# Attention inside a fused block: value products in five visits per group, six banks for the scores, and one bank with fixed places for the rest

## The chip, the cores and the metric

The kernel runs on one core of a Trainium2 chip. The metric is the device time of one execution in microseconds (us). Engines are named as the profile names them: PE is TensorE's matmuls, PEld its weight loads, DVE is VectorE, ACT is ScalarE, POOL is GpSimd and SP is SyncE, which here issues nearly all DMA transfers.

## The reference

One layer over x of shape (1, 2048, 448) computes two branches and mixes them by a gate, all in float32.

```
x = A_x
g = sigmoid((x * gate_w).sum(-1))
a = attention(x): q = x @ wq (16 heads of 28), k = x @ wk, v = x @ wv (one head, shared by all)
    p = softmax(q k^T * 28**-0.5);  o = p v;  a = o @ wo
b = mixer(x): x1 = x + shift(gelu(layernorm(x) @ w1)) @ w2
    b = x1 + gelu(layernorm(x1) @ w3) @ w4
out = g * a + (1 - g) * b
```

## The kernel before

The kernel has three stages. The first projects k and v, computes q for the first two groups, and makes the first half of the mixer. The second is the rest of the mixer, with 56 hidden tiles. Both end some 420 us into the execution and aren't touched by the change. The third is attention, and the change lies there.

**Groups.** The 2048 queries fall into NB = 4 blocks of 512, and the 16 heads into NG = 4 sets of four. A pair of block and set is a group, u = 0 to 15. A group walks NT = 16 key tiles of 128 keys. For each key tile and each of its four heads, one matmul makes scores, keys by queries, 128 x 512, in a PSUM bank (L662), and ScalarE takes the exponential into an SBUF tile p (L664). There are 64 such steps in a group, and this text calls them slots 0 to 63: slot 4 kt + j is head j of key tile kt.

**Value products.** `pv_group(k)` (L617) multiplies the four p tiles of one key tile with the values. Four matmuls, each with 32 output rows, stand side by side in TensorE's array, one per head, and accumulate in one PSUM bank, mx, over the whole group. The weights have a column of ones, so that one output row per head is the softmax's sum. The score loop goes on for two key tiles (LAG = 2) before it does the products of two earlier key tiles in a row (PVB = 2). Such a stretch of value products is called a visit. There are eight visits in a group.

**Other TensorE work of a group**, all between the scores:

- q projection: `q_job(u + 2)` (L492), eleven matmuls of 128 x 512, started in group u at key tile 2. `q_evac` (L144) rounds the result into qh (on ScalarE) and takes the rest ql (on VectorE), and three DMA transfers of 256 KB write qh, ql and qh again into rows 0 to 95 of the tile qs, from which both scores and maxima are made.
- row maxima of a sample of the scores, for group u + 1: `max_part` (L161) four times, each with four matmuls of 128 columns and one reduce on VectorE; they read rows 0 to 95 of qs. `max_end` (L182) and `max_rows` (L190) turn the result, with one matmul and a copy on ScalarE, and two transfers write it into rows 96 and 97 of qs.
- normalisation of the group before: `recip_begin` (L522) copies o out of PSUM on ScalarE, sends the sums through a DMA to a tile rt, checks and inverts them on VectorE, and sends the result back through two DMA transfers (rb). `norm_job` (L540) spreads rb by one matmul, rbc, and multiplies; POOL splits the product into onh and onl.
- the output projection wo: after the fourth group of a block, `wo_job` (L566) runs once for each of its four tiles of 128 queries, with twelve matmuls into one bank, and `gate_out` (L561) applies the gate and stores the tile. For the last block, `wo_last_job` (L638) keeps four banks open in the last group.

These jobs are generators. `pump()` (L600) runs them one matmul at a time after every second score, in the order of the list `jobs`, so where each matmul lands depends on what lies ahead of it in the list. The maxima have fixed places, behind key tiles 6 to 9 and 11.

**Banks.** PSUM has eight banks. Scores rotate over five (mm 2, misc 1, s 2), the value products have one (mx), and the other work has two (m). In the last group the scores use three, because the four open output banks take the rest.

**What sets the order.** PE's order is that of the code: the kernel declares it hand-written (L59). The order on the other engines and of the DMA issues is the compiler's: it takes what it expects to be ready, in the order of the code where several are. Semaphores and the buffers (`bufs`) then decide when something runs. All DMA transfers named here are issued by SyncE on one queue.

```
            if k >= LAG and k % PVB == PVB - 1:
                for kk in range(k - LAG - PVB + 1, k - LAG + 1):
                    if kk >= 0:
                        pv_group(kk)
```

Of the kernel before, what the change touches and what calls it, by code (L numbers as in the profile page):

```python
# [29 lines left out]
LAG = 2  # L30
PVB = 2
# [9 lines left out]
def gated_mix_kernel(  # L41
# [102 lines left out]
    def q_evac(pool, u, ps, qs):  # L144
        qh = pool.tile([P, 512], F32R, tag="qh", bufs=2 if pool.name == "s1" else 1, name=f"qh_{u}")
        ql = pool.tile([P, 512], F32R, tag="ql", bufs=2 if pool.name == "s1" else 1, name=f"ql_{u}")
        nc.scalar.copy(qh, ps)
# [42 lines left out]
    def max_rows(u, tile_of):  # L190
# [4 lines left out]
        nc.scalar.copy(mrow, ps[0:32, :])  # L195
# [196 lines left out]
    with tc.tile_pool(name="s2", bufs=1, reuse_waits="tile") as s2, \  # L392
            tc.tile_pool(name="ps2", bufs=1, space=PSUM, reuse_waits="tile") as ps2:
        fills = [lambda t=t: max_part(0, t, max_tile) for t in range(4)]
        fills += [lambda: max_end(0), lambda: None, lambda: None, lambda: max_rows(0, max_tile)]
# [57 lines left out]
    with tc.tile_pool(name="s3", bufs=1, reuse_waits="tile") as s3, \  # L453
# [23 lines left out]
        def s_tile(n, last=False):  # L477
            return (mm_tile, mm_tile, s_spare, s_more, s_more)[n % (3 if last else 5)](f"s_{n}")
# [13 lines left out]
        def q_job(u):  # L492
# [15 lines left out]
            yield  # L508
# [31 lines left out]
        def norm_job(u, o, rb):  # L540
            ps = (mm_tile if u == NU - 2 else misc_tile)(f"rbc_{u}")
# [3 lines left out]
            onh = s3.tile([P, 512], F32R, tag="onh", bufs=5, name=f"onh_{u}")  # L545
            onl = s3.tile([P, 512], F32R, tag="onl", bufs=5, name=f"onl_{u}")
# [3 lines left out]
            yield  # L550

        def wo_group(ps, b, t, g, first, last):
            tok = slice(t * P, (t + 1) * P)
            onh, onl = on_of[b * NG + g]
            nc.tensor.matmul(ps, onh[:, tok], woh[:, g, :], start=first, stop=False)  # L555
# [3 lines left out]
            nc.tensor.matmul(ps, onl[:, tok], woh[:, g, :], start=False, stop=last)  # L559

        def gate_out(n, ps):  # L561
            ot = s3.tile([P, D], F32, tag="ot", bufs=3, name=f"ot_{n}")
            nc.vector.scalar_tensor_tensor(ot, ps, gg[:, n:n + 1], x1[:, n, :], op0=ALU.mult, op1=ALU.add)  # L563
            nc.sync.dma_start(out[0, n * P:(n + 1) * P, :], ot)

        def wo_job(b, t):  # L566
            ps = misc_tile(f"wo_{b}_{t}")[:, 0:D]
            for g in range(NG):
                yield from wo_group(ps, b, t, g, g == 0, g == NG - 1)
                if g < NG - 1:  # L570
                    yield
            gate_out(4 * b + t, ps)
            yield
# [26 lines left out]
        def pump():  # L600
            if current[0] is None:
                if jobs:
                    current[0] = jobs.pop(0)()
                    next(current[0])
            else:
                try:
                    next(current[0])
                except StopIteration:
                    current[0] = None

        def drain():
            while current[0] is not None or jobs:
                pump()

        p_of, pv_of = {}, {}

        def pv_group(k):  # L617
# [8 lines left out]
            if kt == NT - 1 and u < NU - 1:  # L626
                o, rb = recip_begin(u, pv_of.pop(u))
                delayed.append((k + 6, lambda: norm_job(u, o, rb)))
                if u == NU - 2:
                    for t in range(4):  # L630
                        delayed.append((k + 10, lambda t=t: wo_last_job(t, NG - 2)))
                elif u % NG == NG - 1:
                    for t in range(4):
                        delayed.append((k + 8, lambda t=t: wo_job(u // NG, t)))

        wo_last = []

        def wo_last_job(t, g):  # L638
            if g == 0:
                wo_last.append((m_tile if t < 2 else s_more)(f"wo_{NB - 1}_{t}")[:, 0:D])  # L640
            yield from wo_group(wo_last[t], NB - 1, t, g, g == 0, False)
            yield

        delayed = []
        for k in range(NU * NT + LAG):
            u, kt = divmod(k, NT)
            while delayed and delayed[0][0] <= k:
                jobs.append(delayed.pop(0)[1])
            if k == (NU - 1) * NT:
                for g in range(NG - 2):  # L650
                    for t in range(4):
                        jobs.append(lambda t=t, g=g: wo_last_job(t, g))
            if k < NU * NT:
                if kt == (7 if u == 0 else 2) and u + 2 < NU:
                    jobs.insert(0, lambda u=u: q_job(u + 2))
                if kt == 8 and (u + 3) % NG == 0 and u + 3 < NU:
                    load_x((u + 3) // NG)
                p_of[k] = []
                for j in range(4):
                    n = 4 * k + j  # L660
                    ps = s_tile(n, u == NU - 1)
                    nc.tensor.matmul(ps, kS[0:98, kt * P:(kt + 1) * P], q_of[u][0:98, j, :], start=True, stop=True)  # L662
                    p = s3.tile([P, 512], F32, tag="p", bufs=4 * (LAG + PVB) + 2, name=f"p_{n}")
                    nc.scalar.activation(p, ps, AF.Exp, scale=SCALE)  # L664
                    p_of[k].append(p)
                    if j % 2 == 1 or u == NU - 1:
                        pump()
                if u + 1 < NU:
                    if 6 <= kt < 10:
                        max_part(u + 1, kt - 6, m_tile)  # L670
# [138 lines left out]
```

## Time and profile before

| | |
|---|---|
| median of the runs shown | 1069.96 us (3 runs, 1068.99 to 1070.19) |
| the profiled execution | 1067.96 us, span 1066.2 us |
| first score of the attention stage | 420.57 us into the span |
| first and last copy of o (groups 0 and 14) | 466.4 and 1011.3 us |
| mean granted TensorE clock | 0.987 |
| busy: PE, ACT, DVE, POOL | 98%, 63%, 24%, 14% of the span |

The profile gives one line per group of instructions or, in the timeline, per run of equal instructions: start, duration, engine, line of the code, operation, the tile written and the tiles read, and the count. In brackets stand the idle time of the engine before it and what ended that. Matmuls overlap, so a matmul's duration (0.40 us for 128 x 512) is longer than the distance to the next one. A busy PE is therefore no proof that nothing waits; the distances between starts are. A weight load (PEld) that waits shows a wait of TensorE. In tables of stages the columns are the stretch, its length, the busy time of PE, PEld, DVE, ACT and POOL with their counts, the granted clock, the busy share of the DMA engines and GB/s.

### The profile page before, as it was taken

The numbers are of one execution on the slowest core, as the hardware profiler recorded it, in microseconds if no ns is written. First come the engines' busy times: TensorE is split into PE (matmuls) and PEld (weight loads), VectorE is DVE, ScalarE is ACT, GpSimd is POOL, SyncE is SP. The second block draws the span as 40 slices with busy tenths as digits, with TensorE's granted clock in tenths as the row PEclk, the third lists the DMA queues.
The fourth block names the chain that finished last, engine by engine and source line by source line (L and its number), as shares of the span: only waits on it lengthen the run. The fifth ranks groups of instructions, "written<-read, shape, count | busy, mean of one in ns | idle before, by whom it ended". The sixth has DMA issues, their size and how long they took to land.

```text
span 1066.2 us, 13945 instructions
## 1 busy us (share of the span) xinstructions
PE 1040.3 (98%) x5610; PEld 679.5 (64%) x5610; DVE 258.6 (24%) x528; ACT 673.5 (63%) x1318; POOL 146.1 (14%) x175
## 2 busy tenths in 40 slices
PE   7999989999999999999999999999999999999996
PEld 4787878888888887454554555554655555555442
DVE  6734862411412212301110110120110210111102
ACT  5444462222222223798888888889888888888873
POOL 5622200200200202602000002020002010000100
PEclk8899999999999999999999999999999999999998
DMA  9501330000000001323211202220202220202001
GB/s 312 133 1 37 112 111 1 1 1 1 1 1 1 1 1 61 132 32 70 32 18 15 31 19 41 39 31 3 39 10 41 39 31 2 40 21 30 10 2 38
DMA packets 30541, 41.15 MB, mean 39 GB/s; under 512 B 8004, under 2 KB 20100, under 8 KB 30340
## 3 DMA queue, kind: packets, MB, share of 16 engines
q1 hardware_dynamic: 30324, 40.04, 16.2%
q8 instruction: 46, 0.75, 0.3%
q14 instruction: 27, 0.22, 0.1%
q10 hardware_dynamic: 144, 0.13, 0.0%
HBM read 23.28 MB, written 3.67 MB: 25 GB/s over the span
## 4 chain that ended last, share of the span: by engine, by line
PE 92%; DVE 2%; DMA 2%; ACT 1%; POOL 1%; issue 1%; SPq 0%; POOLq 0%; DVEq 0%; ACTq 0%
PE s L662 27%; PE pv L624 22%; PE acc L418 4%; PE acc L419 4%; PE acc L420 4%; PE g L115 4%; PE g L116 4%; PE g L117 4%; PE q L502 3%; PE m L166 2%; PE wo L559 1%; PE wo L557 1%; PE g L119 1%; PE wo L555 1%; PE g L118 1%; PE h L116 1%
## 5 line engine op out<-in xcount | busy, mean ns | idle before, releaser
L664 ACT ACTIVATE p<-s 128x512 f32<-128x512 f32 x1024 | 517.6, 630 | 99.7 <-PE s L662 99.4
L662 PE MATMUL s<-qs,kS 98*128 98x512 f32 x1024 | 343.5, 420 | 1.4 <-ACT p L664 0.7
L662 PEld LDWEIGHTS s<-qs,kS 98*128 98x128 f32 x1024 | 181.7, 189 | 168.3 <-ACT p L664 126.2
L624 PE MATMUL pv<-p,vext 128*32 128x512 f32 x2048 | 247.5, 601 | 0.0
L408 ACT ACTIVATE gh<-g 128x512 fp32r<-128x512 f32 x56 | 33.6, 599 | 175.0 <-PE g L119 174.9
L624 PEld LDWEIGHTS pv<-p,vext 128*32 128x32 f32 x2048 | 53.7, 109 | 107.5 <-issue 100.1
L410 DVE TENSOR_TENSOR gl<-gf,gh 128x512 fp32r<-128x512 f32 x56 | 38.7, 692 | 183.8 <-ACT gf L409 183.8
L418 PE MATMUL acc<-w4h,gh 128*128 128x448 f32 x224 | 82.8, 370 | 0.0
L419 PE MATMUL acc<-w4l,gh 128*128 128x448 f32 x224 | 82.0, 366 | 0.0
L420 PE MATMUL acc<-w4h,gl 128*128 128x448 f32 x224 | 81.7, 365 | 0.0
L167 DVE TENSOR_REDUCE mr<-m 128x4 f32<-128x512 f32 x64 | 44.2, 691 | 146.8 <-PE m L166 146.1
L115 PE MATMUL g<-ah,w3h 128*128 128x512 f32 x168 | 66.6, 396 | 3.7 <-ACT gf L409 3.7
L116 PE MATMUL g<-al,w3h 128*128 128x512 f32 x168 | 66.3, 395 | 0.0
L117 PE MATMUL g<-ah,w3l 128*128 128x512 f32 x168 | 66.3, 394 | 0.0
L547 POOL CAST onh<-on 128x512 fp32r<-128x512 f32 x15 | 9.2, 614 | 415.0 <-DVE on L544 228.9
L520 DVE SCALAR_TENSOR_TENSOR good<-rt,good 128x16 f32<-128x16 f32 x15 | 2.6, 175 | 190.9 <-DMA rt<-o 190.9
L418 PEld LDWEIGHTS acc<-w4h,gh 128*128 128x128 f32 x224 | 42.2, 188 | 4.9
L419 PEld LDWEIGHTS acc<-w4l,gh 128*128 128x128 f32 x224 | 42.2, 188 | 4.9
L420 PEld LDWEIGHTS acc<-w4h,gl 128*128 128x128 f32 x224 | 42.0, 188 | 3.6
L166 PEld LDWEIGHTS m<-kS,qs 96*128 96x128 f32 x256 | 38.4, 191 | 6.3 <-DVE mr L167 1.2
L115 PEld LDWEIGHTS g<-ah,w3h 128*128 128x128 f32 x168 | 31.7, 188 | 9.9 <-ACT gf L409 4.1
L563 DVE SCALAR_TENSOR_TENSOR ot<-wo,gg,x 128x448 f32<-128x448 f32 x16 | 10.9, 681 | 108.0 <-PE wo L559 107.9
(204 smaller groups left out, 1134.9 us busy)
## 6 DMA issues: line engine op xcount, KB each, us to landing
qs<-qh SPq DMA_DIRECT2D x32, 256.0 KB
qs<-ql SPq DMA_DIRECT2D x16, 256.0 KB
xq<-in_xT_dram SPq DMA_DIRECT2D x4, 1024.0 KB
x<-in_x_dram SPq DMA_DIRECT2D x4, 896.0 KB
w3raw<-in_w_dram SPq DMA_DIRECT2D x7, 512.0 KB
out_dram<-ot SPq DMA_DIRECT2D x16, 224.0 KB
w4raw<-in_w_dram SPq DMA_DIRECT2D x7, 448.0 KB
xkv<-in_xT_dram SPq DMA_DIRECT2D x3, 1024.0 KB
```

Source lines behind the costliest of these rows:

```text
L115: nc.tensor.matmul(ps, wh[:, c, :], ah[:, c, :], start=(c == 0), stop=False)
L116: nc.tensor.matmul(ps, wh[:, c, :], al[:, c, :], start=False, stop=False)
L117: nc.tensor.matmul(ps, wl[:, c, :], ah[:, c, :], start=False, stop=False)
L166: nc.tensor.matmul(ps[:, j, :], q_of[u][0:96, j, t * P:(t + 1) * P], kS[0:96, 0:MK], start=True, stop=True)
L167: nc.vector.reduce_max(mx_of[u][:, :, t], ps, axis=AX.X)
L410: nc.vector.tensor_sub(gl, gf, f32(gh))
L418: nc.tensor.matmul(ps, gh[:, tok], w4h[i][:, k, :], start=(f == 0), stop=False)
L419: nc.tensor.matmul(ps, gh[:, tok], w4l[i][:, k, :], start=False, stop=False)
L420: nc.tensor.matmul(ps, gl[:, tok], w4h[i][:, k, :], start=False, stop=(f == NF - 1))
L624: nc.tensor.matmul(pv[32 * j:32 * j + 32, :], vext[:, kt, :], ps[j], start=(kt == 0), stop=(kt == NT - 1), tile_position=(0, 32 * j))
L662: nc.tensor.matmul(ps, kS[0:98, kt * P:(kt + 1) * P], q_of[u][0:98, j, :], start=True, stop=True)
L664: nc.scalar.activation(p, ps, AF.Exp, scale=SCALE)
```

## The change

The attention stage gets a new order of TensorE's work, new owners for the PSUM banks, and a new place for the output projection.

- Visits: five in a group in place of eight. Behind key tile 0 the last four key tiles of the group before are multiplied, and behind key tiles 3, 6, 9 and 12 three each. In the last group two more visits of two tiles follow, behind key tile 14 and at the end. Twenty-two p tiles in place of eighteen.
- Banks: scores rotate over six banks in every group (mm 2, misc 1, s 3). All other work shares one bank, m.
- Fixed places, by slot: rbc at 16; maxima of the next group at 19, 23, 27 and 35, their rows at 45; the twelve wo matmuls of the group before at 29 to 31, 39 to 41, 47 to 49 and 52 to 54; the q projection of the group after the next at 58, 60, 62 and 63 and, in the next group, at 0 to 3, 5, 7 and 9. Group 0 has its own places.
- q projection: with that, the last q matmul for group u + 1 and its evacuation stand in group u, at slot 9, and the first maximum of group u + 1 at slot 19 of the same group. Before, q of group u + 1 was done in group u - 1.
- Output projection: `wo_job` now runs for every group, three matmuls per query tile, and VectorE adds the gated product to a tile ot that lives over the four groups of a block (five buffers). The store follows the fourth. The last block has no banks of its own any more; in the tail, the first two query tiles share the m bank.
- The copies of q to qh and of the maxima's rows to mrow move from ScalarE to VectorE. The load of the next block's x stands at key tile 3 of the group in which its first q projection starts.

```diff
-            if k >= LAG and k % PVB == PVB - 1:
-                for kk in range(k - LAG - PVB + 1, k - LAG + 1):
-                    if kk >= 0:
-                        pv_group(kk)
+        WO_AT = (29, 30, 31, 39, 40, 41, 47, 48, 49, 52, 53, 54)
+        Q_AT = (58, 60, 62, 63, 0, 1, 2, 3, 5, 7, 9)
+        FIRST_AT = tuple(range(36, 58, 2))
+        M_AT = (19, 23, 27, 35, 45)
+        FIRST_M = (3, 7, 11, 15, 23)
+
+        visits = {0: (-4, 0), 3: (0, 3), 6: (3, 6), 9: (6, 9), 12: (9, 12)}
+        for k in range(NU * NT + 1):
+            u, kt = divmod(k, NT)
+            if k < NU * NT:
+                if kt == (9 if u == 0 else 14) and u + 2 < NU:
+                    jobs.append(q_job(u + 2))
+                if kt == 7 and u > 0:
+                    for t in range(4):
+                        jobs.append(wo_job(u - 1, t))
+                if kt == 3 and (u + 2) % NG == 0 and u + 2 < NU:
+                    load_x((u + 2) // NG)
...
+                    at = 4 * kt + j
+                    if at in (WO_AT + Q_AT if u else FIRST_AT):
+                        pump()
+                    if at == 16 and norms:
+                        norm(*norms.pop())
+                    places = M_AT if u else FIRST_M
+                    if u + 1 < NU and at in places:
+                        t = places.index(at)
+                        if t < 4:
+                            max_part(u + 1, t, m_tile)
+                        else:
+                            max_rows(u + 1, m_tile, nc.vector.tensor_copy)
+                        if t == 3:
+                            max_end(u + 1)
+            lo, hi = visits.get(kt, (0, 0))
+            if u == NU - 1 and kt == 14:
+                lo, hi = 12, 14
+            if u == NU:
+                lo = -2
+            for kk in range(u * NT + lo, u * NT + hi):
+                if kk >= 0:
+                    pv_group(kk)
...
         def m_tile(name):
-            return ps3.tile([P, 512], F32, tag="m", bufs=2, name=name)
+            return ps3.tile([P, 512], F32, tag="m", bufs=1, name=name)
 
         def s_more(name):
-            return ps3.tile([P, 512], F32, tag="s", bufs=2, name=name)
+            return ps3.tile([P, 512], F32, tag="s", bufs=3, name=name)
...
-        def s_tile(n, last=False):
-            return (mm_tile, mm_tile, s_spare, s_more, s_more)[n % (3 if last else 5)](f"s_{n}")
+        def s_tile(n):
+            return (mm_tile, mm_tile, s_spare, s_more, s_more, s_more)[n % 6](f"s_{n}")
...
-        nc.scalar.copy(qh, ps)
+        (nc.scalar.copy if pool.name == "s1" else nc.vector.tensor_copy)(qh, ps)
...
+        def wo_job(u, t, tile_of=misc_tile):
+            b, g = divmod(u, NG)
+            n = 4 * b + t
             tok = slice(t * P, (t + 1) * P)
+            onh, onl = on_of[u]
+            ps = tile_of(f"wo_{u}_{t}")[:, 0:D]
+            nc.tensor.matmul(ps, onh[:, tok], woh[:, g, :], start=True, stop=False)
             yield
             nc.tensor.matmul(ps, onh[:, tok], wol[:, g, :], start=False, stop=False)
             yield
+            nc.tensor.matmul(ps, onl[:, tok], woh[:, g, :], start=False, stop=True)
+            before = x1[:, n, :] if g == 0 else ot_of[n]
+            if g == 0:
+                ot_of[n] = s3.tile([P, D], F32, tag="ot", bufs=5, name=f"ot_{n}")
+            nc.vector.scalar_tensor_tensor(ot_of[n], ps, gg[:, n:n + 1], before, op0=ALU.mult, op1=ALU.add)
+            if g == NG - 1:
+                nc.sync.dma_start(out[0, n * P:(n + 1) * P, :], ot_of[n])
```

More of the change, by code (lines that the diff above doesn't have):

```diff
@@ L29 @@
 SHIFTS = (-1, 1, -2, 2)
-LAG = 2
-PVB = 2
+PB = 22
 MK = 128
@@ L194, in max_rows @@
         mrow = keep.tile([32, P], F32R, tag="mrow", bufs=2, name=f"mrow_{u}")
-        nc.scalar.copy(mrow, ps[0:32, :])
+        copy(mrow, ps[0:32, :])
         for k in range(2):
@@ L544, in norm_job @@
             nc.vector.tensor_mul(on, o, ps)
[L545 to L546 removed]
+            onh = s3.tile([P, 512], F32R, tag="onh", bufs=2, name=f"onh_{u}")
+            onl = s3.tile([P, 512], F32R, tag="onl", bufs=2, name=f"onl_{u}")
             nc.gpsimd.tensor_copy(onh, on)
@@ L549, in norm_job @@
             on_of[u] = (onh, onl)
-            yield
-        def wo_group(ps, b, t, g, first, last):
+        ot_of = {}
+        def wo_job(u, t, tile_of=misc_tile):
+            b, g = divmod(u, NG)
+            n = 4 * b + t
             tok = slice(t * P, (t + 1) * P)
-            onh, onl = on_of[b * NG + g]
-            nc.tensor.matmul(ps, onh[:, tok], woh[:, g, :], start=first, stop=False)
+            onh, onl = on_of[u]
+            ps = tile_of(f"wo_{u}_{t}")[:, 0:D]
+            nc.tensor.matmul(ps, onh[:, tok], woh[:, g, :], start=True, stop=False)
             yield
@@ L600, in pump @@
         def pump():
[L601 to L608, printed above, removed]
+            if jobs or current[0]:
+                current[0] = current[0] or jobs.pop(0)
+                if next(current[0], "done") == "done":
                     current[0] = None
[L611 to L615, printed above, removed]
+        p_of, pv_of, norms = {}, {}, []
         def pv_group(k):
```

85 lines of the change are left out of this document (17 added, 68 removed).

## The prediction

> **What bounds the kernel now.** I read the page first: busy shares, then the chain that ended last.
>
> ```profile
> span 1066.2 us, 13945 instructions
> ...
> PE 1040.3 (98%) x5610; PEld 679.5 (64%) x5610; DVE 258.6 (24%) x528; ACT 673.5 (63%) x1318; POOL 146.1 (14%) x175
> ...
> PE 92%; DVE 2%; DMA 2%; ACT 1%; POOL 1%; issue 1%; SPq 0%; POOLq 0%; DVEq 0%; ACTq 0%
> ```
>
> TensorE carries the chain, so only its own issue slots and what it must wait for can move the time. Next the instructions of L524, one copy of o per group, which give the length of a group, and then the timeline of a stretch inside one.
>
> ```profile
> L524 ACT COPY o<-pv x15: 585/587/587, 466.4 to 1011.3; 128x512 f32<-128x512 f32 x15
> ```
>
> ```profile
> 702.05 0.13 PEld L624 LDWEIGHTS pv<-p,vext 128*32 128x32 f32 x4 [0.30 <-issue]
> 702.48 0.13 PEld L624 LDWEIGHTS pv<-p,vext 128*32 128x32 f32 x4 [0.30 <-issue]
> ...
> 703.45 0.73 PE L662 MATMUL s<-qs,kS 98*128 98x512 f32 x2
> ...
> 703.98 4.03 ACT L664 ACTIVATE p<-s 128x512 f32<-128x512 f32 x8 [0.72 <-PE s L662]
> 704.01 0.40 PE L502 MATMUL q<-alq,wqh 128*128 128x512 f32 x1
> ...
> 706.13 0.39 PE L502 MATMUL q<-alq,wqh 128*128 128x512 f32 x1
> ...
> 706.45 1.92 PE L624 MATMUL pv<-p,vext 128*32 128x512 f32 x16
> ...
> 708.31 0.73 PE L662 MATMUL s<-qs,kS 98*128 98x512 f32 x2
> ...
> 709.82 0.56 PE L166 MATMUL m<-kS,qs 96*128 96x128 f32 x4
> ...
> 710.22 0.67 PE L662 MATMUL s<-qs,kS 98*128 98x512 f32 x2
> ...
> 710.42 0.69 DVE L167 TENSOR_REDUCE mr<-m 128x4 f32<-128x512 f32 x1 [8.37 <-PE m L166]
> ```
>
> A group lasts (1011.3 - 466.4) / 14 = 38.9 us. From 704.01 to 706.13 TensorE starts nine matmuls: 0.235 us each. The value products go in fours, 0.43 apart, two fours per key tile: 0.86 a tile. A visit of two tiles runs from 706.13 to 708.31, 2.18 us, of which 1.72 is products and 0.235 an ordinary pitch; the first two scores behind it take 0.56 instead of 0.47. So a visit costs 0.22 + 0.09 = 0.31 us over its products. Eight exponentials take 4.03 us, 0.48 apart, and ScalarE then idles 0.72: it isn't the bound.
>
> **The change part by part.** The sum is made against the profiled execution, 1067.96 us (its span is 1066.2); the median of the runs shown, 1069.96, lies 2.0 above it.
>
> *TensorE's work.* A group has 64 scores and 11 q matmuls at 0.235 (17.6), 16 key tiles (13.8), four maxima of four matmuls at 0.40 (1.6), one rbc and one mt (0.35), and twelve wo matmuls. Their pitch, and the end of the kernel, stand here:
>
> ```profile
> 1040.26 0.37 PE L559 MATMUL wo<-woh,onl 128*128 128x448 f32 x1
> 1040.47 2.21 PE L662 MATMUL s<-qs,kS 98*128 98x512 f32 x5
> ...
> 1048.04 3.64 PE L624 MATMUL pv<-p,vext 128*32 128x512 f32 x32
> ```
>
> At 0.21 the twelve make 2.5, so 35.9 in all. Eight visits add 2.5: 38.4, which leaves 0.5 of the measured 38.9 to waits. Five visits add 1.55: 37.4. None of these matmuls is dropped; wo only moves from twelve per output tile in later groups to three per tile in the next group.
>
> *Score banks, and ScalarE.* A score must wait for the exponential six scores before it (five before). The nearest rows are a stretch without other work:
>
> ```profile
> 694.17 0.73 PE L662 MATMUL s<-qs,kS 98*128 98x512 f32 x2
> ...
> 694.70 4.03 ACT L664 ACTIVATE p<-s 128x512 f32<-128x512 f32 x8 [0.42 <-PE s L662]
> ...
> 696.33 0.19 PEld L662 LDWEIGHTS s<-qs,kS 98*128 98x128 f32 x1 [0.30 <-ACT p L664]
> ```
>
> An exponential starts 0.53 behind the first score, and the eighth score waits until 0.05 past the end of the third exponential. Call T0 the first score behind the visit of four that ends a group. ScalarE first copies o (0.6), so its exponentials start at T0 + 0.62 + 0.48k. With three q matmuls between, the last two of the next twelve scores are due at about T0 + 3.3 and 3.5 and find their banks at 3.35 and 3.8: some 0.2 us lost. The other stretches hold maxima, wo or eight q matmuls, which keep TensorE behind ScalarE. ScalarE's sum is 64 x 0.48 + 0.6 = 31.3 of 37, so its pauses in a longer visit are covered by TensorE's work; moving the q copy and the mrow copy off it gains nothing of itself.
>
> *One bank for the other work.* rbc at slot 16 and the first maximum at slot 19 are four matmuls apart, 0.94; rbc must finish and on (as long as the reduce, 0.69) must clear the bank, some 1.25: 0.3 lost. Elsewhere four scores and a maximum (1.34) match a reduce with its latencies (0.60 + 0.69). VectorE gets 48 more accumulations, by the reduce's row at most 0.69 each, some 2 a group beside 37 of TensorE: hidden, as are its two new copies. Waits so far: 0.5, and 0.3 small ones by the shortfall above. A group would be 38.2 or 38.3, 0.6 under 38.9; times 14, -8.4.
>
> *Before the first copy of o.* It loses 5: 1.8 of a wait on alq (row below, q now comes later), 1.5 of a slow visit behind it, three visits less up to that copy (0.9) and four scores less (0.9). One price the trace doesn't show: the maxima of group 1 now start at slot 3, and VectorE's casts of wq and x can hold their only bank.
>
> ```profile
> 425.70 0.97 DVE L579 CAST wqh<-wqraw 128x768 fp32r<-128x768 f32 x1 [4.30 <-DMA wqraw<-in_wq_dram]
> ...
> 432.11 1.64 DVE L487 CAST ahq<-xq 128x2048 fp32r<-128x2048 f32 x1
> ...
> 433.98 3.46 POOL L488 TENSOR_TENSOR alq<-xq,ahq 128x1536 fp32r<-128x1536 f32 x1 [1.32 <-PE s L662]
> ```
>
> They last from 425.7 to 433.75. Bounds 0 (the reduces go first) and 5 (a bank held until then); I take 2.5, the middle.
>
> *After the last copy of o.* Before, 36 wo matmuls stood there, now 12: -5.0; one visit less and other small terms, -0.9. The tail's two wo tiles on the one bank: +0.5. Without any new wait: 1067.96 - 8.4 - 5 + 2.5 - 5.9 + 0.5 = 1051.7.
>
> *The q projection moves a group nearer to its use.* This decides. Before, q of group u + 2 ended in group u, and the maxima read it in u + 1. Now its last matmul is at slot 9 of the very group in which slot 19 reads it. Between stand a copy and a subtract, both on VectorE now, and three transfers of 256 KB on SyncE, behind the transfers for the reciprocals:
>
> ```profile
> 698.61 0.73 PE L662 MATMUL s<-qs,kS 98*128 98x512 f32 x2
> 698.75 0.59 ACT L524 COPY o<-pv 128x512 f32<-128x512 f32 x1
> ...
> 699.36 0.62 SPq L526 DMA_DIRECT2D rt<-o  x1
> ...
> 701.29 0.17 DVE L520 SCALAR_TENSOR_TENSOR good<-rt,good 128x16 f32<-128x16 f32 x1 [5.37 <-DMA rt<-o]
> ...
> 701.87 0.17 DVE L534 TENSOR_TENSOR rl<-rr,rh 128x16 fp32r<-128x16 f32 x1
> ...
> 702.62 0.56 SPq L537 DMA_DIRECT2D rb<-rl  x1
> ...
> 711.72 0.65 ACT L147 CAST qh<-q 128x512 fp32r<-128x512 f32 x1
> ```
>
> ```profile
> 712.39 0.59 SPq L149 DMA_DIRECT2D qs<-qh  x1
> ```
>
> ```profile
> 713.00:714.00 1.00, 1.00 (x9) 0.24 (x2) 0.69 (x2) 0.36 (x1) 0.00 (x0) 1.00 0.37 139
> ...
> 718.00:719.00 1.00, 1.00 (x9) 0.26 (x2) 0.10 (x1) 0.32 (x1) 0.00 (x0) 1.00 0.98 113
> 719.00:719.50 0.50, 0.50 (x3) 0.41 (x3) 0.00 (x0) 0.23 (x1) 0.00 (x0) 1.00 0.02 0
> ```
>
> With T0 = 698.61: the check waits for rt until +2.68, rl ends at +3.43, SyncE is free at +4.57. q's last matmul is the eighth behind T0 and ends at about +2.4, so in the order of the code its copy stands behind rl: +3.43 to +4.08, the subtract to +4.8, the first transfer at +4.65. From first issue to quiet transfer engines is 6.6 us (712.39 to 719.0, last but one column). A transfer of 8 KB alone took 1.93 from issue to use (699.36 to 701.29); that plus the 5.5 us in which the three moved their data (from about 713.6) is 7.4, which I take. q has landed at T0 + 12.05. The maximum of slot 19 could start at T0 + 8.4 (twelve scores, three q matmuls and the waits above, 4.2; a visit of three with its entry, 2.7; four scores and rbc, 1.2; the bank, 0.3). TensorE stands 3.7 us, with all later work queued behind it. ScalarE drains its four scores and idles too. Groups 2 to 14 do this, 13 times: q of group 2 is done early, and after group 14 there is none.
>
> Bounds: if VectorE runs the q copy before the check, the first transfer leaves at T0 + 3.1, the reciprocal transfers between them cost 0.3, and the wait is 2.4; if the three take 1.2 longer to land, 4.9. I take 3.7 because VectorE sat idle for rt each time and its rows stand in the order of the code.
>
> The rbc itself is safe: rl's transfer leaves at +4.0 and lands about 1.95 later, +5.96, before slot 16 at about +6.9. The load of x on SyncE and its casts on POOL come after q and wait for its last matmul; three times POOL works on them (3.46 for the largest) before onh, whose reader, the wo of slot 29, stands 6 us behind the maximum: taken as nothing, and at worst 3 us in three groups if onh comes late.
>
> *The clock.* Where TensorE already stood still once, it lost more:
>
> ```profile
> 435.47 0.63 PE L662 MATMUL s<-qs,kS 98*128 98x512 f32 x2
> 437.50 0.50 PE L502 MATMUL q<-alq,wqh 128*128 128x512 f32 x1 [1.40 <-POOL alq L488]
> ...
> 438.32 3.43 PE L624 MATMUL pv<-p,vext 128*32 128x512 f32 x16
> ```
>
> ```profile
> 435.00:440.00 5.00, 3.60 (x22) 1.85 (x24) 1.30 (x2) 2.85 (x6) 4.85 (x3) 0.86 0.38 145
> 440.00:445.00 5.00, 5.00 (x28) 2.86 (x19) 0.69 (x1) 2.64 (x6) 4.57 (x2) 0.80 0.61 210
> ```
>
> Two scores started by 435.7, nothing until 437.50, and the visit behind it took 3.43 instead of 1.92: +1.5, with a granted clock of 0.86 and 0.80. A wait of 3.7 should do the same: 13 x (3.7 + 1.5) = 67.6. The sum is 1051.7 + 67.6 = 1119.3, or 1121 against the median.
>
> The Trainium skill, "TensorE: Matmul & The Clock Gate", section "What's actually happening", drops the clock only after at least one idle window of about 3.4 us. Since a wait of 3.7 seldom covers a whole free-running window, by that rule most waits would cost no clock and the sum would be near 1100. The row above differs from it: a gap of 1.8 us was enough, so I go by the row.
>
> **The rivals.**
> - *The clock holds at these waits.* 1051.7 + 13 x 3.7 = 1100. For it: one instance only stands against it, in a stretch with other gaps. The clock rule of the Trainium skill named above would have it so.
> - *VectorE takes the q copy first*: 1051.7 + 13 x (2.4 + 1.5) = 1102. Its rows can't exclude this, as q is ready 0.3 before rt.
> - *q lands in time, and the kernel is faster*: 1052, or 1054 by the median. It decides at a landing before T0 + 8.4, 6.0 behind q's last matmul. Against it: copy and transfers alone take 0.65 + 7.4, and no row shows the three faster than 6.6.
> - *ScalarE becomes the bound in visits of three and four*: it idled 0.72 behind a visit of two; a further tile adds 0.86 and the sixth bank covers 0.48 of it, so 1.1 behind a visit of three and 1.5 to 2 behind one of four. Four of the one, one of the other and 31.3 make 37.5, TensorE's own figure, so by itself it changes nothing; half a us more at each visit would be 2.5 a group and 1051.7 + 35 = 1087.
>
> **How the numbers follow.** The forecast, wait and clock loss both, with the code's order or nearly so (1105 to 1142): 0.60. Clock holds, or q copy first: 0.26. In time: 0.10, faster. A short wait that cancels the gain, about 17 us of 13 x 1.3: 0.04, mostly within 0.2%, which is about what a measurement of this kernel can tell from no change. Faster 0.11, same 0.02, slower 0.87. High end: 13 x (4.9 + 1.5) gives 1135, 1137 by the median, and the early casts 2.5 more: 1140. The low end, 1080, takes 13 x 2.4 = 31 with the clock held (1083) and the casts at nothing.
>
> **What would show it.** Right: in every group from the third to the fifteenth the first maximum's weight load waits 3 to 4 us for the transfer of qh or ql, ScalarE idles some 3 us there, and the granted clock falls to 0.9 or less in the stretch; groups near 43.5 us; five visits; no ScalarE row for qh or mrow. Wrong: a first maximum that follows its four scores at once and groups of 38 us; or the wait at rbc in its place, if the reciprocals' transfers queue behind q's.

## The result, and the profile after

The changed kernel takes 1176.86 us (median of 4 runs, 1175.91 to 1178.78) beside 1069.67 for the kernel before (4 runs): a ratio of 1.1014, 95% interval 1.1001 to 1.1028. It is slower by 107 us; the prediction was 1121, and its range ended at 1140. The profiled execution took 1175.91 us, with a span of 1174.1.

In the changed kernel the scores stand on L635, their exponentials on L637, the value products on L609, rbc on L540, the maxima's matmuls on L165, and the copies of q on L146 and L147. The page after, its busy times, the granted clock in 40 slices and the chain that ended last:

```profile
span 1174.1 us, 14135 instructions
...
PE 1089.0 (93%) x5610; PEld 712.9 (61%) x5610; DVE 317.2 (27%) x605; ACT 664.9 (57%) x1289; POOL 145.9 (12%) x175
...
PEclk8999999999999989998898897988988989889899
...
PE 81%; DMA 8%; DVE 6%; SPq 2%; issue 1%; ACT 1%; POOL 0%; DVEq 0%; ACTq 0%; POOLq 0%
```

TensorE's share of the chain fell from 92% to 81%, and DMA, which had 2%, has 8. The matmuls are as many as before (5610) but are busy 49 us longer, and the granted clock dips to eight tenths (once to seven) in about half of the last 26 slices, which are attention. The stages of attention, in the columns stretch, length, PE, PEld, DVE, ACT, POOL, clock, DMA share, GB/s:

```profile
423.00:466.00 43.00, 36.77 (x190) 18.85 (x188) 15.95 (x18) 29.40 (x60) 21.74 (x16) 0.88 0.35 120
466.00:505.00 39.00, 38.84 (x227) 20.20 (x227) 7.51 (x16) 32.81 (x68) 1.90 (x2) 1.00 0.16 22
505.05:1119.62 614.57, 559.77 (x3027) 309.80 (x3025) 125.36 (x234) 424.64 (x846) 44.33 (x35) 0.90 0.13 25
1119.62:1174.00 54.38, 46.26 (x259) 21.75 (x258) 9.88 (x32) 36.72 (x78) 1.89 (x2) 0.97 0.06 20
```

Row 1 is group 0, row 2 group 1, row 3 groups 2 to 14, row 4 the rest. A group from 2 to 14 lasts 614.57 / 13 = 47.3 us, where the forecast had 43.5; group 1, whose q was ready long before, lasts 39.0. PE stands idle 614.57 - 559.77 = 54.8 us in row 3, and the granted clock is 0.90: about a tenth of 614.57 us, some 61 us, was not granted. The waits from 420 us on give that idle time (us in total, times, longest):

```profile
PE m L165 <- DMA qs<-qh: 31.5, 13, 3.4
...
PE rbc L540 <- DMA rb<-rl: 23.3, 13, 3.4
```

31.5 + 23.3 is the whole 54.8. So TensorE waits twice in each of 13 groups, on average 1.8 us for the reciprocals at rbc and 2.4 us for q at the first maximum. Groups 2, 6 and 10 wait 3.4 and 3.3 us, the other ten 1.3 and 2.2. Group 7 in the timeline (start, duration):

```profile
755.39 0.62 SPq L148 DMA_DIRECT2D qs<-qh  x1
755.39 0.69 DVE L147 TENSOR_TENSOR ql<-q,qh 128x512 fp32r<-128x512 f32 x1
...
756.00 0.17 DVE L518 SCALAR_TENSOR_TENSOR good<-rt,good 128x16 f32<-128x16 f32 x1
...
756.46 2.78 PE L609 MATMUL pv<-p,vext 128*32 128x512 f32 x24
756.57 0.59 SPq L534 DMA_DIRECT2D rb<-rh  x1
...
757.25 0.57 SPq L535 DMA_DIRECT2D rb<-rl  x1
...
757.87 0.58 SPq L149 DMA_DIRECT2D qs<-ql  x1
758.50 0.60 SPq L150 DMA_DIRECT2D qs<-qh  x1
...
760.97 0.47 PE L540 MATMUL rbc<-rb,sel 128*128 128x512 f32 x1 [1.29 <-DMA rb<-rl]
...
764.25 0.64 PE L165 MATMUL m<-kS,qs 96*128 96x128 f32 x4 [2.12 <-DMA qs<-qh]
...
769.74 3.79 PE L609 MATMUL pv<-p,vext 128*32 128x512 f32 x24
```

VectorE copied q before it checked the sums, so q's first transfer stands ahead of the reciprocals' two in SyncE's queue; those needed 760.97 - 757.25 = 3.7 us from the last issue to use. A visit of three tiles took 2.78 us ahead of the waits; behind the second wait the next one takes 3.79. The clock in that stretch:

```profile
764.00:766.00 2.00, 1.75 (x8) 1.53 (x9) 0.69 (x1) 0.74 (x2) 0.28 (x1) 0.75 0.00 0
766.00:768.00 2.00, 2.00 (x8) 1.72 (x7) 0.69 (x1) 1.50 (x4) 0.00 (x0) 0.50 0.00 0
768.00:770.00 2.00, 2.00 (x11) 1.62 (x13) 0.15 (x1) 1.89 (x4) 0.00 (x0) 0.50 0.00 0
770.00:772.00 2.00, 2.00 (x12) 0.39 (x8) 0.54 (x1) 0.00 (x0) 0.00 (x0) 0.55 0.00 0
```

TensorE works without a gap from 764.25 on and yet runs at half clock from about 765.0 till about 771.8. That is 2 x (0.25 + 0.5 + 0.5 + 0.45) = 3.4 us lost, as much as the two waits themselves (1.29 + 2.12).

### The profile page after: what moved, and what is told of

Read it like the earlier page. It is cut to its first block, busy times and chain, and to the rows that moved or that the text cites. A ratio compares the mean times of both kernels' runs of the same rounds, so it can differ in the third digit from the quotient of the medians.

```text
span 1174.1 us, 14135 instructions
## 1 busy us (share of the span) xinstructions
PE 1089.0 (93%) x5610; PEld 712.9 (61%) x5610; DVE 317.2 (27%) x605; ACT 664.9 (57%) x1289; POOL 145.9 (12%) x175
## 4 chain that ended last, share of the span: by engine, by line
PE 81%; DMA 8%; DVE 6%; SPq 2%; issue 1%; ACT 1%; POOL 0%; DVEq 0%; ACTq 0%; POOLq 0%
PE s L635 21%; PE pv L609 19%; DMA qs<-qh 6%; PE acc L418 4%; PE acc L417 4%; PE acc L419 4%; PE m L165 4%; PE g L114 3%; PE q L501 3%; PE g L116 3%; PE g L115 3%; PE wo L557 1%; PE wo L561 1%; PE wo L559 1%; PE g L117 1%
## 5 line engine op out<-in xcount | busy, mean ns | idle before, releaser
L637 ACT ACTIVATE p<-s 128x512 f32<-128x512 f32 x1024 | 514.5, 649 | 194.4 <-PE s L635 194.4
L635 PE MATMUL s<-qs,kS 98*128 98x512 f32 x1024 | 363.0, 438 | 0.0
L635 PEld LDWEIGHTS s<-qs,kS 98*128 98x128 f32 x1024 | 199.3, 203 | 123.7 <-issue 69.1
L609 PE MATMUL pv<-p,vext 128*32 128x512 f32 x2048 | 259.0, 643 | 0.0
L609 PEld LDWEIGHTS pv<-p,vext 128*32 128x32 f32 x2048 | 61.8, 116 | 142.6 <-issue 140.4
L165 PE MATMUL m<-kS,qs 96*128 96x128 f32 x256 | 52.8, 344 | 38.4 <-DMA qs<-qh 31.5
L165 PEld LDWEIGHTS m<-kS,qs 96*128 96x128 f32 x256 | 51.7, 264 | 55.3 <-issue 37.1
L565 DVE SCALAR_TENSOR_TENSOR ot<-wo,gg,ot 128x448 f32<-128x448 f32 x48 | 32.8, 684 | 165.8 <-PE wo L561 165.7
L146 DVE CAST qh<-q 128x512 fp32r<-128x512 f32 x14 | 9.7, 692 | 153.1 <-PE q L501 153.1
```

The source lines that it names most:

```text
L165: nc.tensor.matmul(ps[:, j, :], q_of[u][0:96, j, t * P:(t + 1) * P], kS[0:96, 0:MK], start=True, stop=True)
L609: nc.tensor.matmul(pv[32 * j:32 * j + 32, :], vext[:, kt, :], ps[j], start=(kt == 0), stop=(kt == NT - 1), tile_position=(0, 32 * j))
```

## The experiments

The theory: q comes too late, and the loss is partly waits and partly the clock that falls behind them. The rivals: the shared bank, the long visits or ScalarE cost the time. In all kernels built from the changed one with q earlier, the scores stand on L637 and the exponentials on L639.

**q a group earlier.** The q projection of group u + 3, not u + 2, starts at the end of group u, and the load of x that it needs moves with it; all places stay.

```diff
-                if kt == (9 if u == 0 else 14) and u + 2 < NU:
-                    jobs.append(q_job(u + 2))
+                if u == 0 and kt == 9:
+                    jobs.append(q_job(2))
+                if kt == 14 and u + 3 < NU:
+                    jobs.append(q_job(u + 3))
...
-                if kt == 3 and (u + 2) % NG == 0 and u + 2 < NU:
-                    load_x((u + 2) // NG)
+                if kt == 3 and (u + 3) % NG == 0 and u + 3 < NU:
+                    load_x((u + 3) // NG)
...
-                    if at in (WO_AT + Q_AT if u else FIRST_AT):
+                    if at in (WO_AT + Q_AT if u else FIRST_AT + Q_AT[0:4]):
```

> The changed kernel with one part undone: the q projection of group u + 3, not u + 2, is started at slot 58 of group u, so q is complete a group before the maxima read it. All places stay. Theory (a group of 47.3 us is 38.4 of work, two waits, for q's and for the reciprocals' transfers, 4.2 together, and 4.7 of halved clock behind them): the wait at the first maximum goes, the wait at rbc stays, as the reciprocals' transfers still queue behind q's first one; groups of 40 to 42, in all 1080 to 1105 us. Rival A (one bank and long visits make the order itself slow, the waits only fill its gaps): groups stay above 44 and the time above 1130.

It took 1114.51 us, ratio 1.0424 (1.0406 to 1.0443): 62 us less than the changed kernel, but 10 above the expected range. The wait at the first maximum is gone; the one at rbc stays. Its total, two groups in the stage table, and rbc in the groups from 512, 805 and 934 us:

```profile
PE rbc L540 <- DMA rb<-rl: 23.5, 13, 3.3
```

```profile
512.00:552.60 40.60, 39.08 (x234) 21.30 (x233) 8.80 (x18) 32.45 (x67) 1.90 (x2) 1.00 0.14 21
...
934.00:979.00 45.00, 43.50 (x234) 24.03 (x233) 8.80 (x18) 32.46 (x66) 1.89 (x2) 0.89 0.17 39
```

```profile
526.37 0.47 PE L540 MATMUL rbc<-rb,sel 128*128 128x512 f32 x1 [1.37 <-DMA rb<-rl]
...
821.68 0.47 PE L540 MATMUL rbc<-rb,sel 128*128 128x512 f32 x1 [3.31 <-DMA rb<-rl]
...
948.45 0.47 PE L540 MATMUL rbc<-rb,sel 128*128 128x512 f32 x1 [1.32 <-DMA rb<-rl]
```

This kernel separates wait and clock. Ten of its groups wait 1.2 to 1.5 us: eight keep the full clock and last some 40.7 us, as in the first row, and two lose it, the one at 934 lasting 45. The three groups that wait 3.3 us all lose it, and last 46.3 to 47.4. So every long wait here lost the clock, and of the short ones some did; their length alone doesn't say which.

**No late transfer at all.** On top of that, rbc moves to slot 27 and the maxima to 16, 20 and 24; in group 0 they go later, behind most of VectorE's casts.

```diff
-        M_AT = (19, 23, 27, 35, 45)
-        FIRST_M = (3, 7, 11, 15, 23)
+        M_AT = (16, 20, 24, 35, 45)
+        FIRST_M = (20, 24, 28, 32, 35)
...
-                    if at == 16 and norms:
+                    if at == 27 and norms:
```

> As k1_q_early, and rbc moves from slot 16 to 27, the maxima to slots 16, 20, 24, 35 and 45, those of group 0 to 20, 24, 28, 32 and 35. Theory: no transfer and no cast is waited for any more, the clock stays at 1.00, groups of 38.3, 1046 to 1056 us, faster than before (1069.7). Rival A: groups of 42 and more, above 1100. Rival B (the visits bring nothing, ScalarE holds the pace): groups of 38.9, 1066 to 1072.

1068.13 us, ratio 0.9994 (0.9985 to 1.0003): no difference from the kernel before. So the late transfers and what follows from them make up the entire loss. But the gain that the visits were to bring isn't there either. Groups 2 to 14, and then idle times of the weight loads at the one bank (from 420 us on):

```profile
503.74:1010.17 506.43, 505.97 (x3016) 274.15 (x3014) 120.24 (x232) 421.81 (x846) 37.91 (x32) 1.00 0.14 26
```

```profile
PEld m L165 <- DVE mr L166: 10.4, 30, 2.8
...
PEld rbc L540 <- DVE mr L166: 6.5, 14, 0.5
...
PEld wo L557 <- DVE mrow L194: 4.0, 14, 0.3
PEld mt L192 <- DVE ot L565: 3.9, 14, 0.3
PEld m L165 <- DVE ot L565: 3.9, 14, 0.3
...
PEld q L501 <- DVE ot L565: 3.4, 12, 0.3
```

The clock is full, TensorE idles 0.5 us in 506, and a group lasts 506.43 / 13 = 39.0, not 38.2. Matmuls overlap, so a short wait doesn't show as an idle PE; it shows at the weight load: each change of hands of the one bank (mrow to wo, ot to mt, ot to the next maximum, ot to q, a reduce to rbc) costs a weight load 0.3 to 0.5 us, in 12 to 14 groups each. In groups 2 to 14 these idle times add up to some 2.2 us a group. The time is the one expected if ScalarE held the pace, but ScalarE is busy for only 421.81 of the 506.43 us, and TensorE for 505.97.

**The same wait, filled with work.** In groups 2 to 14, 17 matmuls whose results are unused stand ahead of rbc, in the kernel without late transfers. TensorE then loses about as much time as in the changed kernel, but is hardly ever idle.

```diff
+                    if at == 27 and 2 <= u < NU - 1:
+                        idle = m_tile(f"idle_{u}")
+                        for _ in range(17):
+                            nc.tensor.matmul(idle, identR, kS[:, 0:512], start=True, stop=True)
```

> As k2_all_early, with 17 idle matmuls of 128x512 (results unused, 0.235 us each, 4.0 us in all) ahead of rbc in groups 2 to 14: TensorE is held up about as long as by the two waits of the changed kernel, but works. Theory: the clock stays at 1.00, and the time is that of k2_all_early plus 13 x 4.0 = 52 us, some 60 to 70 us less than the changed kernel, which is then the price of the clock. Rival C (the waits cost more by what they do to ScalarE and the banks behind them than by the clock): within 20 us of the changed kernel's 1176.9.

1123.23 us, ratio 1.0505 (1.0488 to 1.0522). Groups 2 to 14:

```profile
505.48:1068.46 562.98, 561.74 (x3237) 314.89 (x3235) 120.27 (x232) 421.82 (x846) 37.86 (x32) 1.00 0.12 24
```

The clock stays at 1.00, but for one stretch of 3.41 us in group 14, and a group lasts 562.98 / 13 = 43.3: the 39.0 of the kernel without late transfers and 4.3 for the matmuls put in, about as much as the changed kernel's two waits (4.2). The changed kernel's 47.3 lies 4.0 above it, and 13 x 4.0 = 52 us; in whole times it is 1176.86 - 1123.23 = 53.6. That is about the price of the clock. The two kernels also differ in the places of rbc and the maxima; the groups of the first experiment that kept the clock, 40.7 with a wait of some 1.4, leave some 0.3 us a group for that.

**The code's order for the queues.** The changed kernel with one edit, the copy of q back on ScalarE, where it can't run ahead of the reciprocals on VectorE.

```diff
-        (nc.scalar.copy if pool.name == "s1" else nc.vector.tensor_copy)(qh, ps)
+        nc.scalar.copy(qh, ps)
```

> The changed kernel with one part undone: the copy of q to qh is ScalarE's again. On SyncE's queue the reciprocals' two transfers then stand ahead of q's three, the order that the prediction had taken; in the changed kernel they stand behind the first of q's. Theory: no wait at rbc, one wait of some 4.4 us at the first maximum (8.1 us from first issue to last landing) in place of two of together 4.2, and a clock loss of 3.4 to 5 us behind it: 1165 to 1185 us. Rival F (the loss is due to the reciprocals behind q): under 1140.

1197.28 us, ratio 1.1203 (1.1184 to 1.1223), above the expected range too. Its waits, and group 7:

```profile
PE m L165 <- DMA qs<-qh: 61.3, 13, 5.5
...
PE rbc L540 <- DMA rb<-rl: 10.3, 3, 3.5
```

```profile
761.33 0.17 DVE L518 SCALAR_TENSOR_TENSOR good<-rt,good 128x16 f32<-128x16 f32 x1 [10.52 <-DMA rt<-o]
...
762.15 0.65 ACT L146 CAST qh<-q 128x512 fp32r<-128x512 f32 x1
...
763.30 0.59 SPq L148 DMA_DIRECT2D qs<-qh  x1
...
771.48 1.09 PE L165 MATMUL m<-kS,qs 96*128 96x128 f32 x4 [4.52 <-DMA qs<-qh]
```

Here are the prediction's order and its single wait: rbc doesn't wait except in groups 2, 6 and 10, and the first maximum waits 61.3 / 13 = 4.7 us. The three transfers take 771.48 - 763.30 = 8.2 us from first issue to use. The three groups with both waits last 52.0 us on average, the other ten 47.6; that is 13 us, as much as the time lies above the range. With the reciprocals ahead of q the kernel isn't faster, so their place in the queue isn't the cause by itself.

**Eight visits, in the kernel without late transfers.**

```diff
-        visits = {0: (-4, 0), 3: (0, 3), 6: (3, 6), 9: (6, 9), 12: (9, 12)}
+        visits = {n: (n - 3, n - 1) for n in range(1, NT, 2)}
...
-            if u == NU - 1 and kt == 14:
-                lo, hi = 12, 14
```

> As k2_all_early, but with the eight visits of two key tiles of the kernel before. Theory (0.31 us a visit over its products): 46 visits more, 14 us more than k2_all_early if TensorE holds the pace throughout, 8 to 14 us as part of it lies beside waits for ScalarE. Rival B: no difference beyond 2 us.

1124.87 us, ratio 1.0523 (1.0502 to 1.0544). This tells nothing of the visits, as a new wait came with them; its row of the waits:

```profile
PE wo L557 <- POOL onh L545: 16.5, 15, 1.2
```

With rbc at slot 27 and no long visit behind it, POOL's copy of the normalised o comes too late for the first wo. It bears on the clock, though: in the 11 groups whose only wait is this one, 1.1 us long, 8 lost clock.

**Visits and banks, each alone and both.** To give wo its time back, rbc goes to slot 23 and the third maximum to 27; all places of group 0 shift too. This is the base, and three kernels undo the visits, the banks, or both.

```diff
-        FIRST_AT = tuple(range(36, 58, 2))
-        M_AT = (19, 23, 27, 35, 45)
-        FIRST_M = (3, 7, 11, 15, 23)
+        FIRST_AT = (38, 40, 41, 43, 44, 46, 48, 50, 52, 54, 56)
+        M_AT = (16, 20, 27, 35, 45)
+        FIRST_M = (24, 28, 31, 34, 37)
...
-                    if at == 16 and norms:
+                    if at == 23 and norms:
```

> As k1_q_early, and rbc at slot 23, the maxima at 16, 20, 27, 35 and 45; in group 0 the maxima at 24, 28, 31, 34 and 37 and q at 38 to 56, so that the weight casts on VectorE are over. k2_all_early had groups of 39.0, the same as the kernel before, and lost some 5 us in group 0. Theory (five visits and six banks are worth no more than the one bank costs): groups of 38.9 to 39.1, group 0 some 4 us shorter than in k2_all_early, 1062 to 1066 us. Rival D (k2_all_early still waits somewhere that this order doesn't): groups of 38.3 and 1053 to 1057.

> As k7_five_visits with the eight visits of two key tiles; rbc is early enough here for wo, for which k4_eight waited. Theory: 46 visits more at 0.31 us, partly beside waits for ScalarE: 6 to 14 us more than k7_five_visits, groups of 39.4 to 39.8. Rival B (visits bring nothing): within 2 us.

The banks are undone so (the third kernel; the fourth has both edits):

```diff
-            return ps3.tile([P, 512], F32, tag="m", bufs=1, name=name)
+            return ps3.tile([P, 512], F32, tag="m", bufs=2, name=name)
...
-            return ps3.tile([P, 512], F32, tag="s", bufs=3, name=name)
+            return ps3.tile([P, 512], F32, tag="s", bufs=2, name=name)
...
-            return (mm_tile, mm_tile, s_spare, s_more, s_more, s_more)[n % 6](f"s_{n}")
+            return (mm_tile, mm_tile, s_spare, s_more, s_more)[n % 5](f"s_{n}")
```

> As k7_five_visits, but with the banks of the kernel before: five for the scores, two for the other work. If the one bank's handovers cost some 0.7 us a group (waits of 0.3 for VectorE in front of m, mt, wo and rbc), they go; the scores wait for ScalarE some 1.4 us more in a group, by the bank recurrence of the prediction with five banks. Theory: groups of 39.3 to 39.9, 5 to 14 us more than k7_five_visits. Rival E (the sixth bank brings nothing): 5 to 10 us less.

> As k7_five_visits with both undone, eight visits, and five banks for the scores and two for the rest; only the fixed places and the new wo remain. Theory: near the kernel before, 1066 to 1076 us. If long visits need the sixth bank, the five banks cost less here than in k9_two_m.

Times and the length of an ordinary group (the median of groups 2 to 12, from the starts of their first scores):

| | six score banks, one m | five score banks, two m |
|---|---|---|
| five visits | 1072.90, ratio 1.0033 (1.0019 to 1.0046); 39.1 | 1092.56, 1.0219 (1.0205 to 1.0234); 40.5 |
| eight visits | 1085.57, 1.0162 (1.0134 to 1.0191); 40.1 | 1073.59, 1.0041 (1.0027 to 1.0056); 39.0 |

With six score banks, eight visits cost 1.04 us a group more than five: 0.35 for each of the three, where the prediction had 0.31. (The time is in the expected range, the group a little above it.) With five score banks, long visits cost 1.5 more than short ones, and scores wait for exponentials. The base's row of that wait, and then that of five visits with five score banks (which, 20 us above the base, was to cost 14 at most):

```profile
PEld s L637 <- ACT p L639: 21.6, 76, 0.3
```

```profile
PEld s L637 <- ACT p L639: 85.1, 333, 0.3
```

In the first weight load behind a visit the idle time reads 0.84 us in all four kernels, and with eight visits most of these are put down to the same wait. Without them it is 65 us from 503 to 1010 us in five visits with five score banks, 13 in eight visits with five, and 12 in the base: the wait comes with long visits and five banks together. The one bank's price shows with eight visits: 40.1 with one m, 39.0 with two, although a score bank goes for it. So fewer visits need the sixth bank, the sixth bank leaves one for all else, and what the visits save the single bank takes back. The two old choices together and the two new ones together give the same group, 39.0 and 39.1.

The base missed its expectation (1062 to 1066) in group 0, which lasted 42.9 us:

```profile
441.70 3.96 POOL L586 TENSOR_TENSOR wol<-woraw,woh 128x1792 fp32r<-128x1792 f32 x1
441.78 3.91 DVE L185 SCALAR_TENSOR_TENSOR mc<-mr,mc 128x16 fp32r<-128x16 f32 x1
...
445.83 0.45 PE L192 MATMUL mt<-identR,mc 128*128 128x128 f32 x1 [4.28 <-DVE mc L185]
```

An operation of VectorE on 128 x 16 elements takes 3.91 us while a subtraction of POOL runs, and both end within 0.03 us of each other. TensorE waits for it, 4.28 us.

**The start of attention.** In the kernel without late transfers, the maxima and the q projection of group 0 get places behind VectorE's casts and POOL's subtractions.

```diff
-        FIRST_AT = tuple(range(36, 58, 2))
+        FIRST_AT = tuple(range(46, 57))
...
-        FIRST_M = (20, 24, 28, 32, 35)
+        FIRST_M = (24, 28, 31, 34, 44)
```

> As k2_all_early, with group 0 laid out anew: maxima at slots 24, 28, 31, 34, their rows at 44, q at 46 to 56, behind VectorE's casts and POOL's splits. Theory: group 0 of 38 to 39 us instead of 42.5, the granted clock without its drop there, 1062 to 1066 us.

1061.96 us, ratio 0.9936 (0.9918 to 0.9953), at the lower edge of what was expected. Group 0, and groups 2 to 14:

```profile
422.00:458.78 36.78, 35.65 (x194) 18.80 (x192) 17.22 (x18) 30.99 (x62) 21.80 (x16) 1.00 0.48 149
497.93:1004.17 506.24, 505.81 (x3016) 274.09 (x3014) 120.19 (x232) 421.83 (x846) 37.88 (x32) 1.00 0.14 26
```

Group 0 takes 6.2 us less than in the changed kernel's first row, and the groups are still 506.24 / 13 = 38.9.

**The copy of o on VectorE.** One more edit, to free ScalarE when a group begins.

```diff
-            nc.scalar.copy(o, pv)
+            nc.vector.tensor_copy(o, pv)
```

> As k11_head, with the copy of o out of PSUM on VectorE. In k2_all_early the stretch of slots 12 to 15 takes 4.23 us where its matmuls add up to 3.83: the scores wait for ScalarE, whose exponentials start 0.5 us late behind the copy of o. Theory: 0.3 to 0.4 us a group less, 4 to 6 us under k11_head, 1057 to 1062 us. Rival: the wait there is that of the six banks alone, no change.

1060.15 us, ratio 0.9919 (0.9904 to 0.9933): 1.8 us better, not 4 to 6, and groups 2 to 14 are still 38.9. ScalarE's copy wasn't what keeps the group at 39. Of all kernels run this is the fastest, 9 us below the kernel before.

## Why the prediction was right or wrong

*The sign was right, and the cause in the main.* With q a group earlier 62 of the 107 us go, in 13 groups, as forecast, at the reader and the row named. The rest belongs to a second wait, at rbc, which the sum didn't have; with q early and rbc later the loss vanishes.

*The clock: the step that failed.* "A wait of 3.7 should do the same: 13 x (3.7 + 1.5)" took 1.5 us from the only wait that the trace of before had. That one was 1.4 us long. In the traces' clock records half clock lasts 3.41 us or a multiple of it; behind that wait it lasted one such step (438.59 to 442.00), which costs 1.7. In the changed kernel it lasts two steps in five of the 13 groups, three in five others and four in groups 2, 6 and 10. The comparison with the filled wait gives 4.0 us a group, or, from the third row of the stages, (614.57 - 54.8) / 13 - 39.0 = 4.1. So 2.6 us a group were missing, 33 us of the 57 between forecast and profile (1175.91 against 1119.3). The range failed at the same place: its high end took the longest wait (4.9) but again 1.5 for the clock. One instance gives a size, not a bound.

The weighing with the Trainium skill, "TensorE: Matmul & The Clock Gate", section "What's actually happening", came out on the right side for this kernel, as all 13 groups lose clock. The Trainium skill isn't simply wrong there: eight waits of 1.2 to 1.5 us in the first experiment cost none, as its idle window of about 3.4 us would have it, and two did. It puts the return at about 3.4 us of sustained work; group 7 took 7.6, from 764.25 to about 771.8.

*The order of the queues.* "I take 3.7 because ... its rows stand in the order of the code" was wrong: VectorE took q first. But "The rbc itself is safe" was worked out for the other order only. With q's transfer ahead, the reciprocals wait behind it, and rbc adds 1.8. The last sentence of the prediction named this sign; the sum didn't hold it. The bound given for VectorE's order, 2.4 at the maximum, is the average measured there (31.5 / 13), but by luck: in group 7 (T0 = 752.25) the first transfer left at T0 + 3.1, as the bound has it, and q was there for use at T0 + 12.0, not 10.8, while TensorE came later too, by rbc's 1.29. That the forecast had q landed at T0 + 12.05 is luck as well, and so is the total: 4.2 us of waiting for 3.7, as the two errors nearly cancel. In the code's order (ScalarE's copy) the wait is 4.7, as the transfers land in 8.2 us and not in 7.4.

*POOL's casts of x.* They were "taken as nothing, and at worst 3 us in three groups", for another reason than the one that came. In groups 2, 6 and 10, VectorE's small cast of the reciprocals stands still beside POOL's subtraction. Group 6, in the timeline:

```profile
706.01 3.47 POOL L487 TENSOR_TENSOR alq<-xq,ahq 128x1536 fp32r<-128x1536 f32 x1
706.16 3.35 DVE L531 CAST rh<-rr 128x16 fp32r<-128x16 f32 x1
...
712.38 0.47 PE L540 MATMUL rbc<-rb,sel 128*128 128x512 f32 x1 [3.36 <-DMA rb<-rl]
...
716.95 1.09 PE L165 MATMUL m<-kS,qs 96*128 96x128 f32 x4 [3.40 <-DMA qs<-qh]
```

Those three groups last 50.7, 50.7 and 50.3 us, the other ten 46.3 on average: 13 us together, part of the waits and the clock above.

*The visits and the one bank.* The price of a visit was about right (0.35 for 0.31). The waits that replace them were not: for the "0.3 small ones", which had no row of their own, about 1.1 are left over, and a group without late transfers takes 39.0 and not 38.2 or 38.3. Over 13 groups that is 10 us. Only the handover from rbc to the first maximum was priced, and those among the maxima were taken to fit; wo, mt and q change hands at the same bank. The 1.1 agrees with what a second m bank gave with eight visits (40.1 to 39.0).

*The start and the end.* In group 0 the casts held the bank of the maxima, as feared, but beyond the bound of 5:

```profile
435.27 1.11 PE L165 MATMUL m<-kS,qs 96*128 96x128 f32 x4 [6.23 <-DVE mr L166]
436.31 4.95 PE L609 MATMUL pv<-p,vext 128*32 128x512 f32 x24
```

The wait is 6.23 us, and the visit behind it takes 4.95 where 2.78 is the rule. The bound counted the casts' durations only; again the clock was left out. Up to the first copy of o the kernel loses 5.3 us (471.7 against 466.4) where a gain of 2.5 was forecast; 2.5 of the difference lie before the first score (423.04 for 420.57), in stages that the change leaves alone; the other kernels' traces have it anywhere from 420.2 to 422.3. From the last copy to the end it takes 1174.1 - 1125.3 = 48.8 us instead of 54.9, the forecast -5.4 nearly.

So of the 57 us: clock 33, base of the group 10, waits 7 (54.8 for 48.1), the start 8, the end -1.

*ScalarE as the bound* fell: with q early it idles while TensorE stays full.

What stays open: why the clock stays low for one step in some places and two or more in others, and which short waits drop it. The clock records narrow the second. All changes of the clock in a trace lie on one grid of 3.41 us. Over all these traces, from 150 us on, a step of that grid at full clock in which TensorE was idle for 1.9 us or more was followed by half clock in 33 of 33 cases, one with 0.9 to 1.9 us in 25 of 64. In the changed kernel every drop in the 13 groups follows a step with 1.97 to 2.73 us, both waits added where both lie in it, and no step with 0.55 to 1.50 was followed by one. Idle time isn't all, as the filled kernel's one drop came without any. No run changed only the place of a wait in time.

## What to carry to other kernels

When a producer moves nearer to its reader, add up the whole chain to the reader (copy, queue, landing) for each order that the scheduler may choose, and look at what else is queued on the same DMA queue. A wait of TensorE is paid twice here, once as the wait and about once more as half clock behind it: 4.2 us of waits cost a group 8.3. Single short waits cost less, and often nothing. A gain from fewer, longer stretches of one kind of work is real, but it needs buffers, and the buffers must come from somewhere: test both together and each alone.

## What the runs showed of the hardware that was not expected

- Half clock outlasts the gap. In group 7 it lasted 6.8 us behind gaps of 1.29 and 2.12 us, all of it in uninterrupted work.
- Half clock comes in steps of 3.41 us on a grid: in attention, stretches of one to four steps, and once of five (17.07 us, in group 2 of the kernel with ScalarE's copy of q). In each trace only the stretch that the end of the kernel breaks off is no multiple.
- The length of a short wait doesn't decide whether it costs clock: of ten waits of 1.2 to 1.5 us in the first experiment, eight cost none and two did; of eleven of 1.1 us in the kernel with eight visits and rbc at slot 27, three cost none and eight did.
- VectorE's smallest operations can stand still while POOL runs a subtraction with both inputs in SBUF: a cast of 128 x 16 took 3.35 us in group 6 and 0.18 in group 7. The Trainium skill, "SBUF — State Buffer", section "Who interferes with whom", has this: VectorE's casts can contend with GpSimd for a shared port pair, as can its operations with two inputs in SBUF when GpSimd's reads SBUF, and whoever comes second blocks fully. The trace agrees: the cast ends 0.03 us after POOL's operation.
- Three transfers of 256 KB within SBUF on one queue take 8.2 us from first issue to use, and the second of two small transfers issued behind the first of them takes 3.7 where one took 1.9 alone (699.36 to 701.29 in the trace of before).
